# Loading the attention output in head-by-column rectangles, and setting up the sequence transform earlier, in a four-layer kernel

## The chip, the cores and the metric

The kernel runs on one core of one Trainium2 chip, in one launch. The metric is the device time of that launch in microseconds (us). A core has a matrix engine (TensorE, PE in the profile; its weight loads stand as PEld), three engines for elementwise work (VectorE or DVE, ScalarE or ACT, GpSimd or POOL), a queue that in this kernel issues all the DMA transfers (SyncE, SP), and 16 DMA engines that carry them out. Each engine works through its own list of instructions in order, and waits on semaphores for the others.

## What is computed

The input x is 2048 rows (S) of 640 columns (D). Four layers follow each other, attention and Fourier mixing in turn, each added to its own input:

```python
# attention, with q, k, v = layernorm(x) @ wqkv, 32 heads of 20, window of 256 rows back
scores = einsum("bhqd,bhkd->bhqk", q, k) * (Dh ** -0.5)
p = softmax(where(mask, scores, -1e9))
x = x + merge_heads(einsum("bhqk,bhkd->bhqd", p, v)) @ wo
# Fourier mixing, with n = layernorm(x)
a = einsum("bsd,ed->bse", n, dft_hid_re); b = einsum("bsd,ed->bse", n, dft_hid_im)
x = x + einsum("ts,bse->bte", dft_seq_re, a) - einsum("ts,bse->bte", dft_seq_im, b)
```

Everything is fp32 to the outside. Large products are made from split operands: a value is divided into a rounded high part and the remainder (two fp32r tiles), and three products of parts are added.

## The kernel before

**Heads.** The 32 heads are worked in 8 quads of 4. Rows come in 4 blocks of 512 (`sb` or `bk` in the code) and 16 tiles of 128. `heads()` is one loop of 16 steps a quad. A step issues scores (L505), their exponential on ACT (`t_exp`, L513), the band masks on POOL (`t_mask`, L519 and L523), and the product with the values (L543). `mt` holds row maxima that go into a row of `qp` by DMA before the scores of their quad. When a quad's row block is finished, `finish` copies the accumulators to `ou`, stores them unnormalised to the DRAM tensor `o_d` (head, 32 rows, S), and after a reciprocal stores the inverse sums to `r_d`; the pair (quad, block) is then entered in `stored`.

**The slot clock.** `tick` advances a slot counter, twice in each step. `post(delay, fn)` puts off issuing work by so many slots, so that the order of the instructions on each engine is written by these delays. After the heads, `spend` makes a slot of each 0.65 us of assumed TensorE work. What TensorE does in a step beside the heads is poured in by `fill`: the next quads' projections, then the early part of the output projection (`partials`), then its late part (`late`).

**The output projection.** The contraction of 640 rows is worked in 5 chunks of 128, chunk k being the rows 128k to 128k+127 of an order (quad, column of the head, head in the quad). Chunks 0 to 2 (`EARLY = 3`) are early: they are loaded, multiplied and added to the layer's input while the last quads still run. Chunks 3 and 4 are late. `load_o` brings a chunk of one row block: for each quad that it touches, one load of raw rows from `o_d` (L695) and one broadcast load of inverse sums from `r_d` (L696). It then posts the multiply of the two (L704) and the split into parts (L156 on ACT, L162 on POOL). These posts lie 16 and 19 slots ahead while the heads run, both halves on POOL; after the heads the multiply is on DVE, and they lie 9 and 11 slots ahead.

**The late stage.** `poll_late` loads the weights of the late chunks in the last quad, then calls `late_load` for each row block once it is stored, two at most while the heads run. `late` makes one tile at a time: two accumulations of the late chunks (L169), their sum with the early part on DVE (L830), the row statistics (L183 and after), a power on POOL (L837), and the normalisation on ACT (L813, L814) into the `big` tiles. For the second half of the tiles, `sums` then forms sums and differences of tile j and j + 8 (L885 to L889). `fourier_hook(t)` runs after each tile.

**The sequence transform.** It is worked in units: eight `a1`, eight `a2`, eight `b` and so on, each one tile of rows long. A unit needs a block of the sequence matrix and the split x. `load_to` issues the 512 KB loads of matrix blocks (L934), `cut_to` folds them (POOL L947, DVE L952 and L956) and splits them into the tiles `c`, `qp` and others, and `x_to` splits the x of the next unit just ahead of it (ACT L156, POOL L162; tiles `big`). The products are L1017. `unit` is called between late tiles, when two more tiles than units have been normalised. The buffers are set up by `take_fourier`, which before the change is called at the first late tile. The Fourier layer ends with the transform along the columns, which the change leaves alone.

SP issues all DMAs in program order: the heads' loads, `load_o`'s, the matrix blocks, and the writes of x (L833).

Of the kernel before, what the change touches and what calls it, by code (L numbers as in the profile page):

```python
# [15 lines left out]
P = 128  # L16
# [41 lines left out]
class Net:  # L58
# [392 lines left out]
    def heads(self, xsrc, xdst, hook):  # L451
# [100 lines left out]
        def finish(quad, bk):  # L552
            ou = self.next("ou")
            nc.scalar.activation(ou, acc.pop((quad, bk)), AF.Copy)
            sm = pool.tile([P, 16], F32, name="sm", tag="sm")
            rc = pool.tile([P, 16], F32, name="rc", tag="rc")
            cols = slice(bk * 512, (bk + 1) * 512)
            at = (2, 16, 18) if quad < NQ - 1 else (1, 7, 8)
            self.post(at[0], lambda: nc.sync.dma_start(sm, ou[0:P:32, :]))
            self.post(at[0], lambda: nc.sync.dma_start(  # L560
                self.od[4 * quad:4 * quad + 4, :, cols].rearrange("h r s -> (h r) s"), ou))
            self.post(at[1], lambda: nc.vector.reciprocal(out=rc, in_=sm))

            def store():
                nc.sync.dma_start(
                    self.rd[bk, 4 * quad:4 * quad + 4, :].rearrange("h (a b) -> (h a) b", b=16), rc)
                self.stored.add((quad, bk))
            self.post(at[2], store)
# [48 lines left out]
        for step in range(-LEAD, steps + 2):  # L617
# [25 lines left out]
            for z in range(2):  # L643
# [34 lines left out]
    def load_o(self, o, sb, k, raw=None, rr=None):  # L678

        nc = self.nc  # L680
        raw = self.raw()[:, :512] if raw is None else raw
        for q in range(k * P // 80, (k * P + P - 1) // 80 + 1):
            while (q, sb) not in self.stored:
                if self.heavy:
                    self.relieve()
                self.tick()
        rr = self.next("rr") if rr is None else rr
        cols = slice(sb * 512, (sb + 1) * 512)
        r = k * P
        while r < k * P + P:  # L690
            q, d0 = r // 80, r % 80 // 4
            d1 = min(DH, d0 + (k * P + P - r) // 4)
            n, hs = 4 * (d1 - d0), slice(4 * q, 4 * q + 4)
            rows = slice(r - k * P, r - k * P + n)
            nc.sync.dma_start(raw[rows, :], self.od[hs, 1 + d0:1 + d1, cols].rearrange("h d s -> d h s"))  # L695
            nc.sync.dma_start(rr[rows, :], self.rd[sb, hs, :].unsqueeze(0).broadcast_to([d1 - d0, 4, 512]))  # L696
# [80 lines left out]
    def late_load(self):  # L777
        sb = len(self.late_o)
        o = self.late_set(sb)
        self.late_o.append(o)  # L780
        p = [cuts(t, 512) for t in self.pt]
        raws = (p[3][:2], [p[3][2], None], [p[0][2], p[1][2]], [p[2][2], None])[sb]
        for k, r in zip(range(EARLY, KC), raws):
            self.load_o(o, sb, k, r, self.vq[k - EARLY] if sb == 3 else None)

    def poll_late(self, n):

        if n == 1:
            self.late_w = pairs(cuts(self.qp[0][:, :4 * D], D))
            spare = cuts(self.pt[3], D)  # L790
            self.late_wl = [self.load_w(self.late_w, self.a["wo"], [k], at=k - EARLY, into=spare[k - EARLY])
                            for k in range(EARLY, KC)]
            for f in self.late_wl:
                next(f)
        if n == 4:
            for f in self.late_wl:
# [9 lines left out]
    def late(self, xsrc, xdst, hook):  # L806
# [43 lines left out]
    def after_heads(self):  # L850
        self.after, self.spent = True, 0.0
        for _ in self.out:
            self.spend(0.147)
        self.load_to(4)
        while True:
            t = self.late_t
            self.poll_late(99)
# [23 lines left out]
    def sums(self, j, early):  # L881
        nc = self.nc
        a, b = self.y_part(j), self.y_part(j + NB // 2)
        if early:
            nc.gpsimd.tensor_tensor(out=self.s3[j], in0=a[:, :256], in1=a[:, 384:], op=OP.subtract)  # L885
            nc.gpsimd.tensor_tensor(out=a[:, 384:], in0=a[:, 384:], in1=b[:, 384:], op=OP.add)
        else:
            nc.vector.tensor_tensor(out=a[:, :256], in0=a[:, 384:], in1=a[:, :256], op=OP.subtract)
            nc.vector.tensor_tensor(out=self.s4[j], in0=b[:, :256], in1=a[:, :256], op=OP.subtract)  # L889
            self.normed += 1  # L890

    def unit(self):

# [2 lines left out]
            return False  # L896
        self.seq(n)
        self.un = n + 1
        self.spend(2.7 if self.order[n][2] == "a1" else 1.4)
        return True  # L900

    def take_fourier(self):
        def halves(t):
            return t.rearrange("p (l c) -> p l c", l=2)

        self.xa = [halves(t) for i in (0, 1) for t in cuts(self.take_big(i), 2 * D)]
        w = [self.work.tile([P, 2 * D], F32, name="s3", tag="wc") for _ in range(2)]
        self.s3 = sum([cuts(t[:, :1024], 256) for t in w], [])
        self.raws = [t[:, :1024] for t in w]
# [10 lines left out]
        self.un, self.normed = 0, 0  # L920
        self.acc = {}

    def load_to(self, n):
        while self.n_load <= min(n, len(self.order) - 1):
# [4 lines left out]
                continue  # L929
            m = self.n_raw  # L930
            self.n_raw += 1
            r = self.raws[m] if m < 2 else self.pt[m % 3][:, :1024]
# [33 lines left out]
    def x_to(self, n):  # L966
        nc = self.nc
        while self.n_x <= min(n, len(self.order) - 1):
# [4 lines left out]
            first, pool = u < 4 * NB // 2, nc.gpsimd  # L973

            def parts(x, src, at, eng=None):
                w = src.shape[1]
                self.split(x[:, 0, at:at + w], x[:, 1, at:at + w], src, eng=eng)

            if ph == "a1":
                parts(self.xa[j], a[:, :384], 0, pool)  # L980
            if ph == "a2":
                parts(self.xa[j], a[:, 384:], 384, pool)
            x = [self.xa[j]]
            if ph == "b":
                x = [self.xb[j], self.xm[j % 2]]
                if first:
                    parts(x[0], self.s4[j], 0, pool)
                    parts(x[0], self.s3[j], 256, pool)
                parts(x[1], b[:, 256:384], 0)
            if ph == "g":  # L990
                if first and j == 0:
                    self.xring = [self.work.tile([P, 2, D], F32R, name="xc", tag="wc") for _ in range(2)]
                x = [self.xring[j % 2], self.vq[j % 2].rearrange("p (l c) -> p l c", l=2)]
                parts(x[0], b, 0)
                parts(x[1], a[:, :256], 0)
            self.x_of[u] = x

    def seq(self, n):
# [100 lines left out]

    def fourier_hook(self, t):  # L1100
        if t == 0:
            self.take_fourier()
        if t == 8:
            self.s4 = cuts(self.take_qk("kp", 0, F32)[:, 2048:], 256)
# [30 lines left out]

    def fourier(self, xsrc, xdst, more):
        nc = self.nc
        self.free.extend((5, 6))
        for name, n in (("vq", 2), ("rr", 3)):
            for i in range(n):  # L1140
                getattr(self, name)[i] = self.slot_tile(f"{name}{i}", 512, F32R)
        self.ring.append((self.rr[1], self.rr[2]))
        self.xm = [t.rearrange("p (l c) -> p l c", l=2) for t in cuts(self.rr[0], 256)]
        self.xb = [t.rearrange("p (l c) -> p l c", l=2) for n, i in (("qp", 0), ("kp", 1))
                   for t in cuts(self.take_qk(n, i), 1024)]
# [113 lines left out]
def arrange(A_x, A_wqkv, A_wo, B_dft_seq_re, B_dft_seq_im, B_dft_hid_re, B_dft_hid_im):  # L1259
# [15 lines left out]
    def rows(w):  # L1275
# [11 lines left out]
        "x": f(np.asarray(A_x)[0]),  # L1287
        "wqk": f(wqk),
        "wv": rows(wqkv[:, 2 * D:]),
        "wo": rows(np.asarray(A_wo)[[(4 * q + h) * DH + d for q in range(NQ) for d in range(DH) for h in range(4)]]),  # L1290
        "c": f(c),
        "wr": rows(np.asarray(B_dft_hid_re).T),
        "wi": rows(np.asarray(B_dft_hid_im).T),
# [20 lines left out]
```

## Time and profile before

| what | us |
|---|---|
| median of three runs | 2414.03 (2410.94 to 2416.91) |
| the profiled execution | 2416.66 |
| its span on the chip | 2414.9 |
| mean granted TensorE clock, share of full speed | 0.978 |
| DVE, ACT, POOL busy, share of the span | 65%, 45%, 43% |
| heads of the first attention layer end at about | 605 |
| late tiles and units a1, a2 of the first Fourier layer | about 605 to 700 |
| the same of the second round | about 1815 to 1900 |

Times in the trace are counted from the start of the span. An engine's busy time is given with its number of instructions. A wait is put down to the one that released it. An arrow `out<-in` names the tiles of an instruction without their numbers; `big`, `pt`, `qp`, `kp`, `vq`, `rr` and `ou` are fixed buffers that change their use in the course of the layer.

### The profile page before, as it was taken

The numbers are of one execution on the slowest core, as the hardware profiler recorded it, in microseconds if no ns is written. First come the engines' busy times: TensorE is split into PE (matmuls) and PEld (weight loads), VectorE is DVE, ScalarE is ACT, GpSimd is POOL, SyncE is SP. The second block draws the span as 40 slices with busy tenths as digits, with TensorE's granted clock in tenths as the row PEclk, the third lists the DMA queues.
The fourth block names the chain that finished last, engine by engine and source line by source line (L and its number), as shares of the span: only waits on it lengthen the run. The fifth ranks groups of instructions, "written<-read, shape, count | busy, mean of one in ns | idle before, by whom it ended". The sixth has DMA issues, their size and how long they took to land.

```text
span 2414.9 us, 40687 instructions
## 1 busy us (share of the span) xinstructions
PE 2277.8 (94%) x13584; PEld 1703.6 (71%) x13584; DVE 1579.7 (65%) x3770; ACT 1097.7 (45%) x1853; POOL 1037.6 (43%) x1509
## 2 busy tenths in 40 slices
PE   7999999998899999999999999999888899999999
PEld 6964544455677878789989544445556688787899
DVE  5256676664688879772461667776637888798622
ACT  3125555544555555551121255556445555455410
POOL 4035565755665243330130456657656652242300
PEclk9999999998899999999999999999988999999999
DMA  5545555664434454644536455556644354546543
GB/s 177 180 141 151 167 164 174 186 184 145 155 130 144 147 167 127 216 165 158 170 136 190 142 157 154 172 177 194 187 126 156 129 162 143 172 134 194 185 146 110
DMA packets 219059, 387.13 MB, mean 160 GB/s; under 512 B 39649, under 2 KB 86241, under 8 KB 218849
## 3 DMA queue, kind: packets, MB, share of 16 engines
q1 hardware_dynamic: 218848, 384.53, 50.8%
q8 instruction: 108, 1.77, 0.3%
q14 instruction: 103, 0.84, 0.1%
HBM read 269.48 MB, written 113.77 MB: 159 GB/s over the span
## 4 chain that ended last, share of the span: by engine, by line
PE 65%; POOL 8%; DVE 7%; ACT 7%; DMA 6%; issue 4%; SPq 3%; POOLq 0%; ACTq 0%; DVEq 0%
PE banks L169 30%; PE banks L1017 19%; PE banks L505 7%; PE banks L543 5%; ACT pt L513 4%; PE banks L476 3%; DMA pt<-c 3%; POOL kp L1057 2%; DVE qp L162 1%; POOL big L162 1%; DVE pt L956 1%; POOL pt L947 1%; DVE st L183 1%; POOL pt L519 1%; DMA qp<-qk_d 1%
## 5 line engine op out<-in xcount | busy, mean ns | idle before, releaser
L481 DVE CUSTOM_DVE_ANT_0 ux<-banks,mask 128x384 bf16<-128x384 f32 (+2 forms) x1024 | 544.3, 532 | 244.8 <-PE banks L476 143.4
L513 ACT ACTIVATE pt<-banks 128x768 f32<-128x768 f32 (+2 forms) x512 | 395.0, 771 | 388.8 <-PE banks L505 270.5
L519 POOL TENSOR_SCALAR_AFFINE_SELECT pt<-pt 128x256 f32<-128x256 f32 x512 | 212.9, 416 | 333.7 <-ACT pt L513 326.2
L169 PE MATMUL banks<-big,wc 128*128 128x512 f32 x1200 | 343.6, 417 | 1.2 <-DVE big L162 0.5
L505 PEld LDWEIGHTS banks<-qp,kp 61*128 61x128 f32 x1024 | 101.6, 186 | 272.3 <-ACT pt L513 221.4
L505 PE MATMUL banks<-qp,kp 61*128 61x384 f32 (+2 forms) x1024 | 230.2, 437 | 50.4 <-ACT pt L513 38.1
L169 PEld LDWEIGHTS banks<-big,wc 128*128 128x128 f32 x1200 | 212.2, 191 | 75.1 <-issue 32.1
L162 DVE TENSOR_TENSOR qp<-pt,qp 128x512 fp32r<-128x512 f32 (+1 forms) x226 | 195.9, 886 | 53.1 <-ACT qp L156 51.0
L156 ACT ACTIVATE qp<-pt 128x512 fp32r<-128x512 f32 (+1 forms) x227 | 138.7, 627 | 185.4 <-POOL pt L947 42.1
L543 PE MATMUL banks<-pt,vq 128*32 128x384 f32 (+2 forms) x2816 | 214.3, 402 | 0.0
L476 PE MATMUL banks<-kp,qp 60*128 60x384 f32 (+2 forms) x1024 | 192.9, 344 | 4.8 <-DVE mc L481 4.7
L523 POOL TENSOR_SCALAR_AFFINE_SELECT pt<-pt 128x256 f32<-128x256 f32 x448 | 185.9, 415 | 0.0
L955 POOL TENSOR_TENSOR pt<-pt,pt 128x512 f32<-128x512 f32 x40 | 87.3, 2194 | 224.1 <-ACT c L156 137.6
L1017 PE MATMUL banks<-qp,big 128*128 128x512 f32 x576 | 150.8, 412 | 27.1 <-POOL big L162 9.0
L1200 DVE TENSOR_TENSOR x<-banks,x 128x320 f32<-128x320 f32 x64 | 30.0, 488 | 191.1 <-PE banks L169 105.3
L1017 PEld LDWEIGHTS banks<-qp,big 128*128 128x128 f32 x576 | 112.0, 198 | 58.9 <-POOL big L162 10.9
L156 ACT ACTIVATE c<-pt 128x512 fp32r<-128x512 f32 x184 | 113.6, 626 | 75.5 <-DVE pt L956 38.4
L162 DVE TENSOR_TENSOR c<-pt,c 128x512 fp32r<-128x512 f32 x184 | 143.0, 793 | 2.6 <-ACT c L156 1.4
L476 PEld LDWEIGHTS banks<-kp,qp 60*128 60x128 f32 x1024 | 111.2, 188 | 25.3 <-DVE mc L481 12.0
L1017 PE MATMUL banks<-c,big 128*128 128x512 f32 x468 | 120.0, 402 | 9.5 <-POOL big L162 4.1
L169 PE MATMUL banks<-big,pt 128*128 128x320 f32 x768 | 119.6, 312 | 2.7 <-DVE x L1200 2.7
L1017 PE MATMUL banks<-qp,xc 128*128 128x512 f32 x480 | 117.4, 392 | 4.7 <-DVE xc L162 4.0
(180 smaller groups left out, 4273.0 us busy)
## 6 DMA issues: line engine op xcount, KB each, us to landing
pt<-c SPq DMA_DIRECT2D x188, 512.0 KB
qk_d<-c SPq DMA_DIRECT2D x80, 512.0 KB
kp<-qk_d SPq DMA_DIRECT2D x384, 80.0 KB
qp<-qk_d SPq DMA_DIRECT2D x384, 80.0 KB
kp<-u_d SPq DMA_DIRECT2D x32, 640.0 KB
o_d<-ou SPq DMA_DIRECT2D x64, 256.0 KB
x_d<-x SPq DMA_DIRECT2D x48, 320.0 KB
v_d<-pt SPq DMA_DIRECT2D x16, 768.0 KB
```

The lines of the kernel that those rows point to most:

```text
L156: nc.scalar.activation(hi, src, AF.Copy, scale=-1.0 if neg else 1.0)
L162: (eng or nc.vector).tensor_tensor(out=lo, in0=src, in1=hi.bitcast(F32), op=OP.subtract)
L169: self.nc.tensor.matmul(p, x, y, start=n == 0, stop=n == last)
L476: nc.tensor.matmul(p, qp[quad % 2][b:b + 60, z, qb * P:(qb + 1) * P], kp[quad % 2][b:b + 60, z, k0 * P:(qb + 1) * P], start=True, stop=True)
L481: nc.vector.tensor_tensor_reduce(out=self.ux[:, :n * P], in0=p, in1=self.mask[:, 384 - n * P:], scale=1.0, scalar=NEG, op0=OP.add, op1=OP.max,
L505: nc.tensor.matmul(p, kp[quad % 2][b:b + 61, z, kb * P:(kb + 1) * P], qp[quad % 2][b:b + 61, z, kb * P:(kb + n) * P], start=True, stop=True)
L513: nc.scalar.activation(pt[quad, kb][:, 2 * z:2 * z + 2, :n * P], self.banks[:, 0:2, :n * P], AF.Exp, scale=SCALE)
L519: nc.gpsimd.affine_select(out=t[:, :, 0:P], in_=t[:, :, 0:P], pattern=[[0, 2], [1, P]], compare_op=OP.is_ge, fill=0.0, base=0, channel_mul ...
L523: nc.gpsimd.affine_select(out=t[:, :, 256:384], in_=t[:, :, 256:384], pattern=[[0, 2], [-1, P]], compare_op=OP.is_gt, fill=0.0, base=0, ch ...
L543: nc.tensor.matmul(acc[quad, bk][32 * h:32 * h + 32, (qb - 4 * bk) * P:(e - 4 * bk) * P], vq[:, 96 * (kb % 4) + 21 * h:96 * (kb % 4) + 21 ...
L955: nc.gpsimd.tensor_tensor(out=t1, in0=p, in1=t1, op=OP.subtract)
L1017: nc.tensor.matmul(self.banks[:, bk, :], p, b[q], start=start and m == 0, stop=stop and last and m == 2, skip_group_check=True)
```

## The change

It does four things.

1. A chunk of the contraction is now a rectangle of heads and columns, listed in `CHUNKS`, and the rows of `wo` are put in that order on the host. One load brings the raw rows of a chunk and one the inverse sums; the chunks 0 and 1 have the same heads and share one load of inverse sums. A row block takes 9 loads in place of 24. The chunks 0 and 1 need quads 0 to 3, chunk 2 needs 4 and 5, chunk 3 needs 6 and 7, and chunk 4 needs all of them.
2. The posts come earlier: reciprocal and store of the last quad at 5 and 6 slots (7 and 8 before), multiply and split of a chunk at 10 and 13 slots in the heads (16 and 19), at 6 and 8 after them (9 and 11). A chunk counts as done 3 slots after its split.
3. The transform's buffers and the first two matrix loads are set up at step 4 of the last quad, and the first block is folded and split at step 12.
4. The parts of x for a1 and a2 are made 2 or 4 slots after the normalisation, by `split_x`, and no longer just before the unit. The takes of later tiles move to the last late tile (`take_rest`), and the split for the b units may be issued a little ahead (`xb_to`).

The arithmetic is the same; only the order of the contraction rows differs. The core of the diff:

```diff
+CHUNKS = ((0, 16, 0, 8), (0, 16, 8, 16), (16, 24, 0, 16), (24, 32, 0, 16), (0, 32, 16, 20))
...
-            at = (2, 16, 18) if quad < NQ - 1 else (1, 7, 8)
+            at = (2, 16, 18) if quad < NQ - 1 else (1, 5, 6)
...
-            if step >= steps and self.late_t:
+            if step >= steps:
                 self.load_to(step - steps + 2)
...
-        for q in range(k * P // 80, (k * P + P - 1) // 80 + 1):
+        h0, h1, d0, d1 = CHUNKS[k]
+        for q in range(h0 // 4, h1 // 4):
...
-        while r < k * P + P:
-            q, d0 = r // 80, r % 80 // 4
-            d1 = min(DH, d0 + (k * P + P - r) // 4)
-            n, hs = 4 * (d1 - d0), slice(4 * q, 4 * q + 4)
-            rows = slice(r - k * P, r - k * P + n)
-            nc.sync.dma_start(raw[rows, :], self.od[hs, 1 + d0:1 + d1, cols].rearrange("h d s -> d h s"))
-            nc.sync.dma_start(rr[rows, :], self.rd[sb, hs, :].unsqueeze(0).broadcast_to([d1 - d0, 4, 512]))
-            r += n
+        nc.sync.dma_start(raw, self.od[h0:h1, 1 + d0:1 + d1, cols].rearrange("h d s -> d h s"))
+        if k and CHUNKS[k - 1][:2] == (h0, h1):
+            rr = self.turn.pop(("rr", sb))
+        else:
+            rr = self.next("rr") if rr is None else rr
+            nc.sync.dma_start(rr, self.rd[sb, h0:h1, :].unsqueeze(0).broadcast_to([d1 - d0, h1 - h0, 512]))
+            self.turn["rr", sb] = rr
         o["left"] = o.get("left", 0) + 1
+
+        def done():
+            o["left"] -= 1
 
         def cut():
             self.split(o[k][0], o[k][1], raw, eng=nc.gpsimd)
-            o["left"] -= 1
-        eng, at = (nc.vector, (9, 11)) if self.after else (nc.gpsimd, (16, 19))
+            self.post(3, done)
+        eng, at = (nc.vector, (6, 8)) if self.after else (nc.gpsimd, (10, 13))
...
         if n == 4:
             for f in self.late_wl:
                 next(f)
+            self.take_fourier()
+            self.load_to(1)
+        if n == 12:
+            self.cut_to(0)
...
             if t < NB // 2:
-                self.normed += 1
+                self.post(2, lambda: self.split_x(t, 0, 384))
             else:
                 self.post(2, lambda: self.sums(t - NB // 2, True))
+                self.post(4, lambda: self.split_x(t - NB // 2, 384, 640))
                 self.post(5, lambda: self.sums(t - NB // 2, False))
...
+    def split_x(self, j, c0, c1):
+        self.parts(self.xa[j], self.y_part(j)[:, c0:c1], c0, self.nc.gpsimd)
+        self.normed += 1
...
-            if ph == "a1":
-                parts(self.xa[j], a[:, :384], 0, pool)
-            if ph == "a2":
-                parts(self.xa[j], a[:, 384:], 384, pool)
...
     def fourier_hook(self, t):
         if t == 0:
-            self.take_fourier()
+            self.xa = [p.rearrange("p (l c) -> p l c", l=2) for i in (0, 1) for p in cuts(self.take_big(i), 2 * D)]
...
-        if t < 2:
-            self.load_to(t)
-        if t == AFTER and not self.after:
-            self.cut_to(0)
-            self.x_to(0)
```

More of the change, by code (lines that the diff above doesn't have):

```diff
@@ L686, in load_o @@
                 self.tick()
-        rr = self.next("rr") if rr is None else rr
         cols = slice(sb * 512, (sb + 1) * 512)
-        r = k * P
-        while r < k * P + P:
-            q, d0 = r // 80, r % 80 // 4
-            d1 = min(DH, d0 + (k * P + P - r) // 4)
-            n, hs = 4 * (d1 - d0), slice(4 * q, 4 * q + 4)
-            rows = slice(r - k * P, r - k * P + n)
-            nc.sync.dma_start(raw[rows, :], self.od[hs, 1 + d0:1 + d1, cols].rearrange("h d s -> d h s"))
-            nc.sync.dma_start(rr[rows, :], self.rd[sb, hs, :].unsqueeze(0).broadcast_to([d1 - d0, 4, 512]))
-            r += n
+        nc.sync.dma_start(raw, self.od[h0:h1, 1 + d0:1 + d1, cols].rearrange("h d s -> d h s"))
[5 more added lines that the diff above has]
+            self.turn["rr", sb] = rr
         o["left"] = o.get("left", 0) + 1
+        def done():
+            o["left"] -= 1
         def cut():
             self.split(o[k][0], o[k][1], raw, eng=nc.gpsimd)
-            o["left"] -= 1
-        eng, at = (nc.vector, (9, 11)) if self.after else (nc.gpsimd, (16, 19))
+            self.post(3, done)
+        eng, at = (nc.vector, (6, 8)) if self.after else (nc.gpsimd, (10, 13))
         self.post(at[0], lambda: eng.tensor_tensor(out=raw, in0=raw, in1=rr, op=OP.mult))
@@ L782, in late_load @@
         raws = (p[3][:2], [p[3][2], None], [p[0][2], p[1][2]], [p[2][2], None])[sb]
+        rrs = (None, None, None, self.vq)[sb]
         for k, r in zip(range(EARLY, KC), raws):
-            self.load_o(o, sb, k, r, self.vq[k - EARLY] if sb == 3 else None)
+            self.load_o(o, sb, k, r, rrs and rrs[k - EARLY])
     def poll_late(self, n):
@@ L853, in after_heads @@
             self.spend(0.147)
-        self.load_to(4)
+        self.load_to(4 if self.late_t <= 8 else 6)
         while True:
@@ L889, in sums @@
             nc.vector.tensor_tensor(out=self.s4[j], in0=b[:, :256], in1=a[:, :256], op=OP.subtract)
-            self.normed += 1
+    def split_x(self, j, c0, c1):
+        self.parts(self.xa[j], self.y_part(j)[:, c0:c1], c0, self.nc.gpsimd)
+        self.normed += 1
     def unit(self):
@@ L898, in unit @@
         self.un = n + 1
+        if self.late_t == NB and n >= NB // 2 + 4:
+            self.xb_to(n - NB // 2 - 3)
         self.spend(2.7 if self.order[n][2] == "a1" else 1.4)
@@ L904, in halves @@
             return t.rearrange("p (l c) -> p l c", l=2)
-        self.xa = [halves(t) for i in (0, 1) for t in cuts(self.take_big(i), 2 * D)]
         w = [self.work.tile([P, 2 * D], F32, name="s3", tag="wc") for _ in range(2)]
         self.s3 = sum([cuts(t[:, :1024], 256) for t in w], [])
-        self.raws = [t[:, :1024] for t in w]
+        self.raws = [t[:, :1024] for t in w + [self.pt[2], self.pt[0], self.pt[1]]]
         p = [cuts(t, 512) for t in self.pt]
@@ L919, in take_fourier, with take_rest, parts, xb_to @@
         self.free = deque([0, 1, 2, 3, 4, 7])
-        self.un, self.normed = 0, 0
+        self.un, self.normed, self.n_xb = 0, 0, 0
         self.acc = {}
+    def take_rest(self):
+        self.free.extend((5, 6))
+        for name, n in (("vq", 2), ("rr", 3)):
+            for i in range(n):
+                getattr(self, name)[i] = self.slot_tile(f"{name}{i}", 512, F32R)
+        self.ring.append((self.rr[1], self.rr[2]))
+        self.xm = [t.rearrange("p (l c) -> p l c", l=2) for t in cuts(self.rr[0], 256)]
+        self.xb = [t.rearrange("p (l c) -> p l c", l=2) for n, i in (("qp", 0), ("kp", 1))
+                   for t in cuts(self.take_qk(n, i), 1024)]
+    def parts(self, x, src, at, eng=None):
+        w = src.shape[1]
+        self.split(x[:, 0, at:at + w], x[:, 1, at:at + w], src, eng=eng)
+    def xb_to(self, n):
+        while self.n_xb < min(n, NB // 2):
+            j = self.n_xb
+            self.n_xb += 1
+            self.parts(self.xb[j], self.s4[j], 0, self.nc.gpsimd)
+            self.parts(self.xb[j], self.s3[j], 256, self.nc.gpsimd)
     def load_to(self, n):
@@ L931, in load_to @@
             self.n_raw += 1
-            r = self.raws[m] if m < 2 else self.pt[m % 3][:, :1024]
+            r = self.raws[m] if m < len(self.raws) else self.pt[m % 3][:, :1024]
             lo = {"a1": 0, "a": 0, "b": 512, "g": 1024}[ph]
@@ L972, in x_to @@
             a, b = self.y_part(j), self.y_part(j + NB // 2)
[L973 to L977, printed above, removed]
-            if ph == "a1":
-                parts(self.xa[j], a[:, :384], 0, pool)
-            if ph == "a2":
-                parts(self.xa[j], a[:, 384:], 384, pool)
+            first = u < 4 * NB // 2
             x = [self.xa[j]]
@@ L986, in x_to @@
                 if first:
-                    parts(x[0], self.s4[j], 0, pool)
-                    parts(x[0], self.s3[j], 256, pool)
-                parts(x[1], b[:, 256:384], 0)
+                    self.xb_to(j + 1)
+                self.parts(x[1], b[:, 256:384], 0)
             if ph == "g":
@@ L993, in x_to @@
                 x = [self.xring[j % 2], self.vq[j % 2].rearrange("p (l c) -> p l c", l=2)]
-                parts(x[0], b, 0)
-                parts(x[1], a[:, :256], 0)
+                self.parts(x[0], b, 0)
+                self.parts(x[1], a[:, :256], 0)
             self.x_of[u] = x
@@ L1101, in fourier_hook @@
         if t == 0:
-            self.take_fourier()
+            self.xa = [p.rearrange("p (l c) -> p l c", l=2) for i in (0, 1) for p in cuts(self.take_big(i), 2 * D)]
         if t == 8:
-            self.s4 = cuts(self.take_qk("kp", 0, F32)[:, 2048:], 256)
-        if t < 2:
-            self.load_to(t)
-        if t == AFTER and not self.after:
-            self.cut_to(0)
-            self.x_to(0)
+            kp = cuts(self.take_qk("kp", 0, F32), 1024)
+            self.s4 = cuts(kp[2], 256) + cuts(kp[3], 256)
+            self.raws += kp[:2]
+            if self.after:
+                self.load_to(6)
+        if t == NB - 1:
+            self.take_rest()
     def load_u(self, g, part):
@@ L1137, in fourier @@
         nc = self.nc
[L1138 to L1145, printed above, removed]
         wc = pairs(sum([cuts(t, D) for t in self.big[:2]], []) + cuts(self.qp[0][:, :4 * D], D))
@@ L1289, in arrange @@
         "wv": rows(wqkv[:, 2 * D:]),
-        "wo": rows(np.asarray(A_wo)[[(4 * q + h) * DH + d for q in range(NQ) for d in range(DH) for h in range(4)]]),
+        "wo": rows(np.asarray(A_wo)[[h * DH + d for h0, h1, d0, d1 in CHUNKS for d in range(d0, d1) for h in range(h0, h1)]]),
         "c": f(c),
```

## The prediction

> **What bounds the kernel now.** I read the page's engine list and slices first, then the waits of TensorE (PE) between two times, then the chain of waits there, then a table by stage.
>
> From the page, parts 1 and 2 (busy time of each engine; busy tenths in 40 slices, 60.4 us each):
> ```profile
> PE 2277.8 (94%) x13584; PEld 1703.6 (71%) x13584; DVE 1579.7 (65%) x3770; ACT 1097.7 (45%) x1853; POOL 1037.6 (43%) x1509
> ...
> PE   7999999998899999999999999999888899999999
> ...
> PEclk9999999998899999999999999999988999999999
> ```
> PE is the bound nearly everywhere. Its weak places are slices 10 and 11 (about 545 to 665 us) and, in the second attention layer, 29 to 32: the end of the heads, the late output projection, and the start of the sequence transform. The granted clock falls there too.
>
> What PE waited for from 480 to 720 us (total us, times, longest):
> ```profile
> PE banks L1017 <- ACT big L156: 6.6, 3, 3.2
> PE banks L1017 <- POOL big L162: 6.3, 3, 2.2
> PE banks L505 <- ACT pt L513: 4.6, 10, 2.1
> PE banks L169 <- POOL kp L162: 3.3, 3, 1.8
> PE banks L505 <- DMA qp<-mt: 2.7, 1, 2.7
> PE banks L476 <- DVE mc L481: 2.4, 1, 2.4
> PE banks L169 <- ACT kp L156: 1.5, 1, 1.5
> ```
> L1017 is the sequence transform, `big` the split halves of x; L169 with `kp` the late projection, whose operand is split too late; L505 the scores, which once wait for `mt`, a DMA late in SP's queue.
>
> The chain that ended last, 629 to 651 us (start, us, what):
> ```profile
> 631.05 3.90 DMA pt<-o_d
> ...
> 635.26 0.32 SPq L565
> ...
> 636.10 0.68 SPq L695
> ...
> 636.83 0.65 SPq L696
> ...
> 642.99 0.75 SPq L696
> ...
> 643.86 5.69 DMA pt<-c
> ...
> 649.72 1.27 POOL ou L947
> ```
> SP issues one row block's ten loads from 636.10 to 643.74. Only then may it issue the matrix load on which the fold on POOL (L947) and the next unit wait: SP, a queue with no arithmetic, is on the path.
>
> The table by stage (PE, PEld, DVE, ACT, POOL busy; clock):
> ```profile
> 620.00:640.00 20.00, 18.16 (x88) 15.55 (x88) 17.44 (x36) 13.05 (x22) 12.17 (x13) 0.86 0.63 196
> 640.00:660.00 20.00, 12.36 (x44) 9.32 (x44) 12.66 (x21) 8.67 (x16) 13.60 (x11) 0.83 0.48 155
> 660.00:680.00 20.00, 19.73 (x101) 17.50 (x100) 14.72 (x40) 10.84 (x18) 13.50 (x17) 0.92 0.17 66
> 680.00:700.00 20.00, 15.38 (x63) 11.56 (x64) 17.71 (x40) 12.25 (x23) 16.04 (x21) 0.83 0.40 129
> 700.00:720.00 20.00, 19.56 (x86) 15.66 (x86) 18.76 (x26) 12.29 (x31) 9.87 (x13) 1.00 0.48 158
> ```
> From 620 to 700 DVE is busy 62.5 of 80 us and POOL 55.3: little slack behind PE's gaps.
>
> **The change part by part.** Instructions on PE, DVE, ACT and POOL stay the same in number and size; SP loses 120 DMAs (60 in each attention layer). So the forecast is of waits, layer 1 first; layer 2's rows are of the same kind.
>
> (a) *One load per chunk.* An issue of a piece takes .57 to .90 us on SP whatever its rows (16 rows .65, 64 rows .58, 80 rows .77). A late row block falls from ten issues to four, 7.6 to about 3 us; the early ones from 14 to 5. A plain 128-row DMA costs .35 to .48, so the new ones should not cost more than .9. Freed: the `mt` wait (2.7) and the longest L505 wait (2.1), which follows a 3.25 us wait of POOL for the sums of early chunk 2 at 540.66. In layer 2 these are 2.9 and 1.25. Two layers: 9.0 us, from both sides 0 to 9.0. I take 9.0: SP is far enough ahead once it has 9 issues a block instead of 24.
>
> (b) *The last quad earlier:* reciprocal and store 2 slots sooner, multiply and split 6 sooner on POOL (3 on DVE). It frees the waits on `kp`, 3.3 + 1.5 us, layer 2 3.2 + 1.5. PE also runs slowly after a wait: 7 matmuls took 2.66 us at 599.12 and 30 took 6.96 at 620.62 where .147 us each is usual, 1.6 and 2.5 us too many. 8.9 us a layer, 17.8 in two; from 0 to 17.8. I take all of it: six slots of the heads are over 10 us, and the operand is late by 2.5. The added `done` post, 3 slots after the split, is only a guard and delays the tile by less than what the split gains.
>
> (c) *x split at its normalisation, matrix block set up in the last quad.* Eight a1 splits and eight a2 splits (one ACT and one POOL instruction each, 1.14 and .85 us on POOL) go to 2 or 4 slots after their normalisation. They pass SP's row loads, POOL's folds (1.3 to 1.75 each) and the sums (.77, .85). The first fold and its ACT and DVE cuts (one POOL, two ACT, two DVE) move from about 620 to 600 us, into POOL's masks; two 512 KB loads move from 598 and 610 to about 563. There POOL is busy 26 of 40 us and DVE 13, which covers them; without that cover they are 1.3 + 2 x .8 us. PE's waits at stake: 6.6 + 6.3, .8 for `c` and .4 more, 14.1 us, plus slow matmuls (7 in 3.25, 10 in 4.64, 16 in 5.54 at .227 us each: 5.9 us too many). That is 20 us, but 62.5 us of DVE work cannot run in 60. At the .94 that DVE reaches at 700:720 it needs 66.5, so at most 13.5 us a layer are to be had. POOL at its best here (16.04 of 20) needs 69: 10.9. An in-order queue seldom holds its best for 70 us; I take 7, about halfway between nothing and 13.5. Two layers: 14, from 0 to 27.
>
> (d) *What the new shape costs in landing.* The 16-row piece issued at 636.10 arrived in the trace's packet record as 16 packets of 2 KB from 637.59 to 638.2, in four chains, one packet about every 84 ns: four engines, one for each of its four dims. The new last chunk is 4 dims x 32 heads. On four chains that is 32 packets each, 2.7 us, and its sums as much again. Issued third and fourth, it lands about 8.5 us after SP began, against 5.4 with all engines. The DVE multiply comes only 6 slots after, so late blocks 2 and 3 may hold DVE up to 3.1 us each. From 0 (slots took up to 13 us for 9 before) to 6.2 a layer; I take 3, so 6 us in two layers. The Trainium skill, "DMA: Bandwidth & Descriptors", section "Why a DMA increments its semaphore by 16 and not by 1", says that a DMA uses the largest number up to 16 that divides both sides' slowest dimension, and so speaks against this shape; the four chains agree with it. By that rule the price is the one just given; were all 16 engines used, it would be 0 and the sum 6 us lower.
>
> Sum: the profiled execution took 2416.66 us (span 2414.9, 1.8 around it), 2.6 above the median of 2414.03. 9.0 + 17.8 + 14 - 6 = 34.8 us off: 2382.
>
> **The rivals.**
> *A, all waits go:* DVE keeps .94 and landing costs nothing: 9 + 17.8 + 27 = 53.8, so 2363; with DVE's cap broken by 6 us a layer, 2351. For it: at 700:720 DVE does so. Against: POOL's 10.9.
> *B, DVE and POOL bind the late stage:* what PE gains before 620 us it waits for afterwards; left are (a) and the bare waits of (b), 9.0 + 9.5 - 6 = 12.5: 2404. For it: DVE waits 19.5 us for PE in 600:700 but is at 17.4 to 17.7 of 20 twice.
> *C, slower: multiplies before their loads have landed.* POOL's multiply at +10 (was +16) or DVE's at +6 stands in an in-order queue ahead of masks, splits and bank reads. The row at 540.66 (3.25 us of POOL, 2.1 us of PE) is the price; there are 12 such places a layer, 8 early and 4 late. Twelve are 25.2 us a layer against 20.4 of gains before (d): 2416.7 + 9.6 = 2426. It decides from 10 places in 12. For it: early chunk 2 already waits, and would land about when its multiply comes (532 against 531.5 us); against it: the first two early sets land some 4 us ahead.
> *D, the issue grows with rows:* one load costs what its pieces did. (a) is gone and (b) halves; 8.9 + 14 - 6 = 17: 2400. Against it: issue times of 16 to 80 rows are alike.
>
> **How the numbers follow.** My forecast .45 (2370 to 2396), A .16, B .16, D .05, C .18. Within 0.3% (7 us, about what a measurement can tell) lie the milder cases of C and the worst of B, .06; slower has the rest of C, .14; faster .80. The range leaves out A's end below 2355 and C's above 2417.
>
> **What would show it.** In the changed kernel's profile: issue rows of the o_d and r_d loads at .6 to .9 us; no PE wait on `mt`; PE's waits on `kp` (L169) under 1 us; L1044 (L1017 before) with waits on `big` at half or less; `qp` on ACT no longer 8.5 us late for `pt<-c`; DVE over .85 from 620 to 680; PEclk without an 8 in slice 11. I am wrong if POOL or DVE show idle time before the multiply (L708) with a DMA named, above all at 500 to 600 us; if an issue takes over 1.2 us; or if the stage is as long as before with PE waiting for `x` banks instead.

## The result, and the profile after

The changed kernel takes 2393.19 us (median of four runs, 2390.9 to 2394.85) against 2415.14 before (median of four, 2410.94 to 2416.91). The ratio is 0.9907, with a 95% interval of 0.9888 to 0.9925: about 22 us faster. The forecast was 2382, with a range of 2355 to 2417: the sign is right, the gain is two thirds of the one forecast. The profiled execution has a span of 2390.2 us.

The page of the changed kernel, parts 1 and 2 (busy time of each engine, busy tenths in 40 slices):

```profile
PE 2255.3 (94%) x13584; PEld 1690.1 (71%) x13584; DVE 1576.5 (66%) x3770; ACT 1097.4 (46%) x1853; POOL 1034.8 (43%) x1509
...
PE   7999999989889999999999999999898899999999
...
PEclk9999999999899999999999999999999999999999
```

The weak slices at the two transitions are still there. Four slices showed a low clock before (10, 11, 30 and 31); one still does (11). What PE waited for from 470 to 700 us, with lines moved by the change (L508 was L505, L1044 was L1017, L172 was L169):

```profile
PE banks L508 <- ACT pt L516: 11.0, 17, 2.1
PE banks L1044 <- DVE qp L165: 6.1, 2, 5.4
PE banks L1044 <- ACT c L159: 4.7, 1, 4.7
PE banks L1044 <- ACT qp L159: 2.2, 1, 2.2
PE banks L1044 <- ACT big L159: 2.1, 1, 2.1
...
PE banks L1044 <- POOL big L165: 0.4, 1, 0.4
```

All that the change aimed at is gone or small: no wait for `mt` (2.7 before), none for `kp` (3.3 + 1.5), and the units' waits for `big` fall from 12.9 to 2.5 us. In their place stand other waits: for the matrix blocks in `qp` and `c`, and longer ones for the exponentials. Added up over the rows of the waits view, PE's waits have hardly changed: 29.2 us before and 28.8 after from 480 to 720 us, 30.4 and 30.9 from 1660 to 1910 us. What fell is PE's busy time, from 2277.8 to 2255.3 us for the same 13584 matmuls; that is 22.5 of the 24.7 us by which the span is shorter. The mean granted clock rose from 0.978 to 0.986, and 2277.8 times 0.978 / 0.986 is 2259, so by this estimate most of it goes with the clock. What raised the clock no run here separates from the waits.

The waits of all engines from 600 to 650 us say where the matrix blocks were held up:

```profile
ACT qp L159 <- DMA pt<-c: 9.2, 2, 8.1
ACT kp L159 <- DVE pt L708: 7.6, 2, 5.0
DVE pt L708 <- DMA rr<-r_d: 7.5, 2, 5.0
...
DVE x L708 <- DMA vq<-r_d: 4.3, 1, 4.3
```

DVE, which is in the multiply (L708), waits for its loads to land, 11.8 us in this stage. Before, it waited for none here; most of its waiting from 600 to 650 us was for PE (total, times, longest):

```profile
DVE x L830 <- PE banks L169: 15.5, 6, 6.2
```

The chain that ended last goes through that landing (start, us, what):

```profile
615.79 0.55 SPq L692
...
616.38 12.66 DMA rr<-r_d
...
629.17 0.70 DVE pt L708
...
629.89 0.64 ACT kp L159
...
630.60 1.29 POOL kp L165
631.89 9.90 DMA pt<-c
```

Before, ten issues on SP held up the next matrix block until 643.86. Now SP is done with the first row block's loads at 616.9, but the inverse sums of chunk 4 take 12.66 us from issue to landing. The matrix load behind the second row block is issued at 631.89 instead of 643.86; in the wide version below it is issued at 619.91. Two paths end there within half a microsecond: the chain shown, and SP itself, which stood still until 630.06 (last section) and then had three loads to issue first. The DMA view from 625.5 to 629 us, while DVE stands still:

```profile
DMA  1421222222222222122322221222222212221222
...
q1 hardware_dynamic: 183, 0.33, 25.6%
```

The digits are the busy tenths of the 16 DMA engines: 25.6% of 16 is four engines, so twelve are idle on average. What the four carry is the rest of chunk 4's load and, by the packet sizes, the rest of x writes (2560 bytes a packet). The table by stage (PE, PEld, DVE, ACT, POOL busy, clock, DMA share, GB/s) shows the same gap in DVE's time:

```profile
600.00:620.00 20.00, 18.45 (x120) 15.03 (x121) 16.70 (x48) 16.77 (x28) 18.12 (x22) 1.00 0.64 201
620.00:640.00 20.00, 14.59 (x62) 12.12 (x60) 8.92 (x15) 5.95 (x10) 9.60 (x8) 0.83 0.61 185
640.00:660.00 20.00, 16.36 (x68) 13.32 (x67) 17.55 (x33) 11.99 (x21) 14.18 (x13) 0.83 0.22 88
```

### The profile page after: what moved, and what is told of

Read it like the earlier page. It is cut to its first block, busy times and chain, and to the rows that moved or that the text cites. A ratio compares the mean times of both kernels' runs of the same rounds, so it can differ in the third digit from the quotient of the medians.

```text
span 2390.2 us, 40465 instructions
## 1 busy us (share of the span) xinstructions
PE 2255.3 (94%) x13584; PEld 1690.1 (71%) x13584; DVE 1576.5 (66%) x3770; ACT 1097.4 (46%) x1853; POOL 1034.8 (43%) x1509
## 4 chain that ended last, share of the span: by engine, by line
PE 63%; POOL 9%; DMA 9%; ACT 8%; DVE 6%; issue 4%; SPq 1%; POOLq 0%; ACTq 0%; DVEq 0%
PE banks L172 28%; PE banks L1044 19%; PE banks L508 7%; ACT pt L516 5%; PE banks L546 5%; DMA pt<-c 3%; PE banks L479 3%; DMA rr<-r_d 2%; POOL kp L1084 2%; DMA x<-x_d 1%; DVE qp L165 1%; POOL pt L522 1%; POOL pt L526 1%; ACT qp L159 1%; POOL x L708 1%
## 5 line engine op out<-in xcount | busy, mean ns | idle before, releaser
L172 PE MATMUL banks<-big,wc 128*128 128x512 f32 x1200 | 343.6, 417 | 1.2 <-DVE big L165 0.5
L508 PEld LDWEIGHTS banks<-qp,kp 61*128 61x128 f32 x1024 | 100.7, 184 | 274.4 <-ACT pt L516 230.8
L508 PE MATMUL banks<-qp,kp 61*128 61x384 f32 (+2 forms) x1024 | 227.5, 432 | 56.0 <-ACT pt L516 49.7
L172 PEld LDWEIGHTS banks<-big,wc 128*128 128x128 f32 x1200 | 212.2, 191 | 75.0 <-issue 32.1
L1044 PE MATMUL banks<-qp,big 128*128 128x512 f32 x576 | 152.1, 413 | 24.7 <-DVE qp L165 15.2
L1044 PEld LDWEIGHTS banks<-qp,big 128*128 128x128 f32 x576 | 111.9, 198 | 56.8 <-DVE qp L165 20.1
L1044 PE MATMUL banks<-c,big 128*128 128x512 f32 x468 | 122.7, 407 | 17.1 <-ACT c L159 8.7
L1044 PE MATMUL banks<-qp,xc 128*128 128x512 f32 x480 | 117.5, 392 | 3.9 <-DVE xc L165 3.6
L172 PE MATMUL banks<-big,pt 128*128 128x320 f32 x768 | 118.1, 309 | 2.2 <-DVE x L1220 2.2
```

The source lines that it names most:

```text
L172: self.nc.tensor.matmul(p, x, y, start=n == 0, stop=n == last)
L508: nc.tensor.matmul(p, kp[quad % 2][b:b + 61, z, kb * P:(kb + 1) * P], qp[quad % 2][b:b + 61, z, kb * P:(kb + n) * P], start=True, stop=True)
L1044: nc.tensor.matmul(self.banks[:, bk, :], p, b[q], start=start and m == 0, stop=stop and last and m == 2, skip_group_check=True)
```

## The experiments

The time of each is the median of its runs, with the ratio to the kernel before run beside it on the same chip and the interval of that ratio. The medians of the kernel before lay between 2415 and 2418 in these sessions, so gains are taken from the ratios, times 2415; for the changed kernel that gives 22.5 us. The intervals are 0.15 to 0.4% wide on each side (3.5 to 10 us), and small differences are read with that in mind. The edits move the lines: L708 of the changed kernel is L713 in the wide versions, and L1044 is L1049 there.

### Is it the spread of the load over DMA engines?

My theory after the result: the row order (column first, head second) makes chunk 4's load one of 4 slow rows, and it is carried by four DMA engines; the rival was that the DMA engines are all full at that time. The first edit (the wide version) turns the order of rows in the chunks of 16 or more heads:

```diff
-        nc.sync.dma_start(raw, self.od[h0:h1, 1 + d0:1 + d1, cols].rearrange("h d s -> d h s"))
+        src, sums = self.od[h0:h1, 1 + d0:1 + d1, cols], self.rd[sb, h0:h1, :]
+        if h1 - h0 >= 16:
+            sums = sums.unsqueeze(1).broadcast_to([h1 - h0, d1 - d0, 512])
+        else:
+            src, sums = src.rearrange("h d s -> d h s"), sums.unsqueeze(0).broadcast_to([d1 - d0, h1 - h0, 512])
+        nc.sync.dma_start(raw, src)
...
-            nc.sync.dma_start(rr, self.rd[sb, h0:h1, :].unsqueeze(0).broadcast_to([d1 - d0, h1 - h0, 512]))
+            nc.sync.dma_start(rr, sums)
```

The rows of `wo` follow on the host.

> The changed kernel with one edit: in the chunks of 16 or more heads (0, 1 and 4) the row order is head first, column second, so that the slowest dimension of their loads is 16 or 32 and no longer 8 or 4. Same bytes, same number of loads, same posts. Theory (the load is spread over as many DMA engines as its slowest dimension allows, and the 4-engine load of chunk 4 is what DVE waits for): the waits of DVE before the multiply (2.6, 5.0 and 4.3 us in the first late stage) fall under 1 us each, POOL's early waits (0.2 to 1.9 us) shrink too, and the time falls by 10 to 20 us from 2393, to about 2378. Rival (the DMA engines are simply full at that time with the 512 KB and 320 KB transfers, and the spread makes no difference): the waits stay at 2 us or more and the time stays at 2390 to 2396. Second rival (DVE and POOL are the bound): the waits go, but the time stays at 2388 to 2394.

Measured: 2376.56 us (2373.44 to 2382.82), ratio 0.9823 (0.9804 to 0.9842), 42.7 us off. The waits of DVE for these loads from 600 to 690 us shrink to one:

```profile
DVE pt L713 <- DMA rr<-r_d: 1.3, 1, 1.3
```

and the chain from 612 to 645 us no longer holds a load of inverse sums; in its place stands the small write of inverse sums before it (`r_d<-rc`, 6.73 us). The waits do not all fall under 1 us as expected (1.3 us here, 2.3 in the second layer), but the theory stands: same bytes, same number of DMAs, same posts, and some 20 us less; the rival of full engines falls. The second rival, a bound by DVE and POOL, falls as far as the 20 us go.

The next two are variants of the wide version. One turns chunk 4 alone:

```diff
-        if h1 - h0 >= 16:
+        if h1 - h0 >= 32:
```

> As the run before, but only chunk 4 is head first; chunks 0 and 1 keep 8 columns as their slowest dimension. Theory: most of the gain is in chunk 4, so the late waits of DVE go and the early waits of POOL stay: 2393 less 8 to 15, about 2382. Rival (full DMA engines): 2390 to 2396.

Measured: 2382.26 us (2376.55 to 2383.45), ratio 0.9836 (0.9817 to 0.9854), 39.6 us off, as the theory had it. DVE's waits for these loads from 600 to 660 us are 2.9 us, less but not gone; POOL's early waits stay (3.8 us from 470 to 600).

The other turns chunks 0 and 1 alone:

```diff
-        if h1 - h0 >= 16:
+        if h1 - h0 == 16:
```

> The wide version with chunk 4 alone put back to column first, four columns slowest. Theory (chunk 4's load on four DMA engines is what DVE waits for in the late stage): DVE's waits before its multiplies are back at 2 to 5 us each and the time rises by 6 to 14 us from 2376.6, to about 2387. Rival (chunk 4 mattered only because the loads of chunks 0 and 1 filled the same engines): 2375 to 2381.

Measured: 2387.78 us (2378.7 to 2393.59), ratio 0.9882 (0.9841 to 0.9923), 28.5 us off, again as the theory had it. Its DVE waits in the late stage are those of the changed kernel:

```profile
DVE pt L713 <- DMA rr<-r_d: 6.1, 2, 5.0
DVE x L713 <- DMA vq<-r_d: 5.0, 1, 5.0
```

The four make a square. Turning chunk 4 is worth 17 us with chunks 0 and 1 narrow (22.5 to 39.6) and 14 with them wide (28.5 to 42.7). The intervals leave about 6 us on each side of the first difference and 11 of the second. Turning chunks 0 and 1 is worth 6 and 3, within the intervals. So the price of the shape lies in chunk 4, at about 8 us a layer.

### What each part is worth

> The kernel before with part 1 alone: rectangles, one load each, in the shape of the change; all posts, the set-up of matrix blocks and the x split as before. Theory (one load each relieves SP): the wait for mt goes, and the time falls by 4 to 9 us from 2415, to about 2408; with longer posts the slow landing of chunk 4 is mostly covered. Rival (the slow landing eats the gain by itself): 2413 to 2420.

The edit is the loads alone, put into the kernel before:

```diff
-        while r < k * P + P:
...
+        nc.sync.dma_start(raw, self.od[h0:h1, 1 + d0:1 + d1, cols].rearrange("h d s -> d h s"))
...
         eng, at = (nc.vector, (9, 11)) if self.after else (nc.gpsimd, (16, 19))
```

Measured: 2411.53 us (2404.97 to 2413.12), ratio 0.9963 (0.9945 to 0.9982), 9 us off. The wait for `mt` is gone, as the theory had it. But the late stage is no better:

```profile
PE banks L1016 <- ACT big L157: 8.7, 3, 5.3
PE banks L1016 <- POOL big L163: 6.3, 3, 2.3
```

The narrow shape has its price even with the posts of before, when DVE waits only 0.4 us for these loads (600 to 700 us). The wide form of the same part shows it:

> The kernel before with part 1 alone in the wide form. Theory (at 9 slots the slow landing costs a part of what it costs at 6): faster than part 1 alone in the shape of the change, 2411.5 on this measure, by 3 to 8 us, about 2406. Rival (with the posts of before the landing is covered): the same as that, within 3 us.

The edit, against the loads alone:

```diff
-        nc.sync.dma_start(raw, self.od[h0:h1, 1 + d0:1 + d1, cols].rearrange("h d s -> d h s"))
+        src, sums = self.od[h0:h1, 1 + d0:1 + d1, cols], self.rd[sb, h0:h1, :]
+        if h1 - h0 >= 16:
+            sums = sums.unsqueeze(1).broadcast_to([h1 - h0, d1 - d0, 512])
...
+        nc.sync.dma_start(raw, src)
```

Measured: 2390.26 us (2387.87 to 2391.4), ratio 0.9886 (0.9869 to 0.9903), 27.5 us off, about 19 more than the narrow form and far more than the 3 to 8 expected. One load each, well spread, gains by itself as much as the whole change.

> The changed kernel without part 1 and without the earlier posts: loads in pieces of one quad and posts as before, but matrix blocks set up in the last quad and x split at its normalisation. Theory (the parts add up): only the gain of the third and fourth part is left, 8 to 14 us of 2415, so about 2404. Rival (the late stage is held by SP's ten loads a row block, so that the earlier split gains nothing without part 1): 2412 to 2417.

The pieces of the kernel before and all its posts are put back. Parts 3 and 4 stay, and of part 2 only the guard of 3 slots after the split.

```diff
-            at = (2, 16, 18) if quad < NQ - 1 else (1, 5, 6)
+            at = (2, 16, 18) if quad < NQ - 1 else (1, 7, 8)
...
+        while r < k * P + P:
...
-        eng, at = (nc.vector, (6, 8)) if self.after else (nc.gpsimd, (10, 13))
+        eng, at = (nc.vector, (9, 11)) if self.after else (nc.gpsimd, (16, 19))
```

Measured: 2407.5 us (2406.03 to 2408.93), ratio 0.9948 (0.9933 to 0.9962), 12.6 us off: the parts of set-up and x split, without the rectangles. The rival, that they gain nothing while SP is held by ten loads a row block, falls. The gains overlap, though: on top of the wide loads (27.5 us) these parts and the earlier reciprocal bring only some 3 us more, within the intervals (30.7 us, the run after next).

> The changed kernel with the multiply and the split of a chunk put back to 16 and 19 slots in the heads and 9 and 11 after them. Theory (the few-engine loads of chunk 4 land late, and the earlier posts make DVE meet them): DVE's waits of 2.6, 5.0 and 4.3 us before its multiplies get shorter, POOL's early waits go, but the waits of PE for kp (3.3 + 1.5 us a layer) come back; the time stays within 5 us of 2393. Rival (the earlier posts are a gain of 8.9 us a layer by themselves, as the prediction had it): 2405 or more. Second rival (the earlier posts are a net loss in this shape): 2386 or less.

```diff
-        eng, at = (nc.vector, (6, 8)) if self.after else (nc.gpsimd, (10, 13))
+        eng, at = (nc.vector, (9, 11)) if self.after else (nc.gpsimd, (16, 19))
```

Measured: 2402.33 us (2401.05 to 2408.76), ratio 0.9943 (0.9922 to 0.9964), 13.8 us off, between the theory (within 5 us of 2393) and the first rival (2405 or more); the second rival, a net loss, falls. DVE's waits before its multiplies are down to 0.3 us, and PE's for `kp` are back at 2.8 + 0.4 us a layer (none in the changed kernel, 3.3 + 1.5 before; the earlier reciprocal and store stay in this run). Together the earlier multiply and split are worth about 9 us in two layers, with some 7 us of uncertainty.

> The wide version (head first in chunks 0, 1 and 4) with the posts of before, 16 and 19, 9 and 11. Theory (with the loads landing early, the earlier posts are worth the waits for kp and the slow matmuls behind them): slower than the wide version's 2376.6 by 6 to 16 us, about 2387. Rival (the posts do not matter once the loads are wide): 2373 to 2380.

The edit is that of the run before, on the wide version. Measured: 2384.82 us (2381.01 to 2396.31), ratio 0.9873 (0.9843 to 0.9903), 30.7 us off: 12 worse than the wide version, as the theory expected, though the two intervals nearly touch.

The last two runs also say how the price of the narrow shape is paid. With the posts of before DVE does not wait for chunk 4 (0.3 us narrow, none wide), and yet the narrow shape of all chunks costs 17 us (13.8 against 30.7), about as much as with the early posts (20, from 22.5 to 42.7); with the loads alone it costs 18.5 (9 against 27.5). So DVE's wait is not what the time hangs on. Another thing that differs is SP, which stands still until a small write of inverse sums has landed, since its next load reads them. First the narrow run, then the wide one, from 595 to 660 us:

```profile
SPq L697 <- DMA r_d<-rc: 5.8, 1, 5.8
...
SPq L702 <- DMA r_d<-rc: 1.5, 1, 1.5
```

ACT then waits 12.2 us for matrix blocks in the narrow run and 0.9 in the wide one (595 to 660 us):

```profile
ACT qp L159 <- DMA pt<-c: 12.2, 2, 10.9
...
ACT qp L159 <- DMA pt<-c: 0.9, 1, 0.9
```

From SP's start on the first late row block to the matrix load behind the second it takes 16.8 us narrow and 12.0 wide here, 16.5 and 12.2 with the early posts (chunk 4 narrow against the wide version). That is 4 to 5 us of the 8 a layer; where the rest lies stays open.

### A way past both, and what the early posts cost

> The wide version, with chunk 1's multiply and split in the heads 3 slots later (13 and 16), so that POOL no longer has two multiplies of 1.3 us back to back ahead of its masks. Theory (PE's waits for the exponentials, ACT pt, 6.3 us in eight places from 480 to 560 us, come from masks held behind two multiplies): the waits fall by half, and the time by 4 to 8 us in two layers, to about 2371. Rival (each multiply costs the same wait wherever it stands): 2374 to 2379.

```diff
-        eng, at = (nc.vector, (6, 8)) if self.after else (nc.gpsimd, (10, 13))
+        eng, at = (nc.vector, (6, 8)) if self.after else (nc.gpsimd, (10, 13) if k != 1 else (13, 16))
```

Measured: 2379.41 us (2373.89 to 2385.38), ratio 0.984 (0.9812 to 0.9869). PE's waits for `pt` from 480 to 720 us are 8.4 us against 7.6 in the wide version. From 480 to 560 us they are 7.1 against 6.3. The theory falls: taking the two multiplies apart gains nothing that these runs show.

> The wide version with the earlier multiply and split (10 and 13 slots) for the late chunks 3 and 4 alone; the early chunks 0 to 2 keep 16 and 19. Theory (the earlier posts win the waits for kp, and lose part of it again in the early chunks, where PE's waits for ACT pt rose by 3.7 us a layer: 9.4 us in the wide version against 5.7 with the posts of before): 2376.6 less 4 to 8, about 2370. Rival (the early posts neither win nor lose): 2374 to 2380. Second rival (early chunks that come sooner also let their tiles be made sooner): 2381 or more.

```diff
-        eng, at = (nc.vector, (6, 8)) if self.after else (nc.gpsimd, (10, 13))
+        eng, at = (nc.vector, (6, 8)) if self.after else (nc.gpsimd, (10, 13) if k >= EARLY else (16, 19))
```

Measured: 2372.46 us (2368.81 to 2378.02), ratio 0.9824 (0.9794 to 0.9854). The waits behave as the theory says; this line is from 480 to 720 us, against 9.2 us in the changed kernel and 7.6 in the wide version:

```profile
PE banks L508 <- ACT pt L516: 3.4, 12, 0.5
```

The time does not settle it: the median is 4 us lower than the wide version's, but its kernel before was 3 us lower too, and the ratios are equal. Either of the two is faster than the changed kernel by some 20 us.

## Why the forecast was right in sign and too large

- *The sum as a whole.* It counted each wait that goes as time won. The waits that it named went, but by the profile others took their place almost one for one (29.2 and 28.8 us, 30.4 and 30.9), and what was won shows as faster matmuls at a higher granted clock. The forecast priced slow matmuls only as 8.3 us in (b), and in the figures behind (c). That the time came out near it is in part luck.
- *(a), one load per chunk, 9.0 us.* The issues cost what was said: .53 to .65 us in 9 of 11 rows of the changed kernel (483 to 495 and 613 to 632 us), .87 at most, for 128 rows each. The `mt` wait went. Alone and in the shape of the change, loads and landing together gave 9 us where the sum had 9.0 - 6; that near agreement is of two errors. Spread well, the same part gave 27.5: joining the loads was worth far more than the two early waits which the forecast priced. The likely reason is the late sets, which in the chain before stood ahead of a matrix block; the forecast showed that chain, and then priced nothing from it.
- *(d), the landing, 0 to 6.2 us a layer, 3 taken.* This is the term that was mis-sized: 6 us in two layers were taken, and turning chunk 4 was worth 14 to 17. That the load would run on four engines was right and written down; its size and its path were not. The load was put at 8.5 us after SP's start on a row block; it began at 613.94 and landed at 629.04, 15.1 us later. The sum counted 64 packets in a row on each of four engines and left out what stands ahead of them: two 512 KB matrix loads issued at 612.39 and 613.48, and x writes after them. In the packet records, 4 KB packets of the matrix loads keep 12 to 16 engines busy from 614.5 to 618, and only from then on do the 2 KB packets of the row loads come in numbers; 2560-byte packets of x writes run among them until 631. DVE's waits were 7.5 + 4.3 us in the first late stage and 4.8 + 4.0 in the second, past the bound of 6.2 in both. But the forecast let the landing cost only what DVE waits for it, and gave nothing to the delay of what SP issues next. With later posts DVE's wait was 0.3 us and the narrow shape still cost 17.
- *(b), the last quad earlier, 17.8 us.* The waits for `kp` all went, as forecast, yet putting the multiply and the split back cost only 9 us (12 in the wide version; the earlier reciprocal stayed). Part of the gain came back in the heads. PE's waits for the exponentials rose from 4.6 to 9.2 us in the first layer (480 to 720 us) and from 6.9 to 11.4 in the second (1660 to 1910). With the early chunks' posts put back in the wide version they are 3.4 and 3.1. The forecast knew that POOL holds masks behind an early multiply, and gave it only to rival C.
- *(c), x split and set-up, 14 us.* Without the rectangles it measured 12.6. The waits for `big` fell by 10.4 us in the first layer, as far as the forecast said, but they are partly replaced: `c` holds PE once for 4.7 us at the end of a2, and in the wide version for 4.0. That wait is 4.0 in the run without the rectangles too, and does not stand in the runs with the loads alone, so it came with these parts. What stands behind it was not tried.
- *The cap of DVE.* The forecast kept 7 of 13.5 us, since DVE would be near its limit. From 620 to 640 us DVE was busy only 8.92 of 20 us in the changed kernel, waiting for loads. In the wide version it is at 17.56, 18.56 and 16.84 of 20 from 600 to 660: there the limit is near.
- *The rivals.* C, the forecast's slower side, had its multiplies ahead of their loads come true: DVE waited 11.8 us for them in the first late stage, POOL 3.0 us in all at L708 from 470 to 600 us. But with the multiplies put back DVE's wait was gone and the time rose by 9 us, so these waits are not what made the gain small. The row at 540.66 from which C took its price names `qp<-qk_d` as what POOL waited for, not the sums. B, 2404, came as near to 2393 as the forecast, 11 us, but DVE was not at its limit: it stood waiting. A, 2363, is the rival nearest to the wide version's 2377, 14 us away. D fell: issues of 128 rows took no longer than those of pieces.
- *What would show it.* Right: issue times, `mt`, `kp`, `big`. Wrong: `qp` on ACT still waits 9.2 us for `pt<-c` (8.5 before), DVE is at .73 from 620 to 680 us and not over .85, and slice 11 still has an 8 for the clock. The sign of being wrong that the forecast named, DVE idle before the multiply with a DMA named, is there with 11.8 us.

By the Trainium skill, "DMA: Bandwidth & Descriptors", section "Why a DMA increments its semaphore by 16 and not by 1", a DMA takes the largest number of engines up to 16 that divides the slowest dimension of both sides. The runs agree: with 4 columns slowest, 25.6% of 16 engines were busy in the 3.5 us in which the load's last packets ran, and with 32 heads slowest in chunk 4 alone DVE's wait fell from 11.8 to 2.9 us.

## What to carry to other kernels

When several small loads are joined into one, look at the order of its dimensions: here the one with 4 columns slowest left twelve DMA engines idle at its end and cost some 15 us, and swapping two dimensions (and the rows of the weight) gave it back. A load that is slow by its own packets is slower still behind large loads on the same engines: price its landing from the chain, with what was issued just before it, and then price what is issued after it. And where the chain passes through a queue of issues, price the work that stands behind it, not only the waits which a bound engine shows elsewhere.

## What was not expected of the hardware

One load of 256 KB whose slowest dimension is 4 took 12.66 us from issue to landing. A 512 KB matrix load took 5.69 us in the kernel before, 9.90 us in the changed kernel behind such loads, and 5.32 us at the same place in the wide version. In that time SP stood still for 6.6 us. Its next load of inverse sums reads what a small `r_d` write stores, and so it waits for that write:

```profile
SPq L697 <- DMA r_d<-rc: 6.6, 1, 6.6
```

The write is issued at 618.19, behind the narrow loads, and is 128 packets of 64 bytes. In the packet records 96 of them run by 621.4 us; the other 32, a quarter as for four engines of sixteen, run between 626.5 and 629.5, when only about four engines are busy. With chunk 4 alone turned, SP's wait for the write falls from 6.6 to 2.1 us in the first layer and from 5.4 to 2.1 in the second. So a narrow transfer also delays small transfers that were issued after it, and with them the queue that waits for them.
